# Attention with beacons and a max-out feed-forward on one core: a new order of the opening, behind the first weight's request

## The chip, the cores and the metric

The kernel runs on one core of a Trainium2 chip. The time is the device time of one launch in microseconds; a time for a kernel is the median of several launches. A profile is one more execution of the same program, taken by the hardware profiler; its span is counted from the first to the last recorded instruction and is a little shorter than the time measured around it.

## The reference

```python
B, H, S, Nb, D = 8, 8, 576, 16, 64            # q, k, v, beacon_k, beacon_v: float32
k_all = concat([beacon_k, k], axis=2)          # 16 beacons ahead of the 576 keys
v_all = concat([beacon_v, v], axis=2)
scores = q @ k_all.T / sqrt(D)                 # per batch and head
scores[:, Nb:] is masked causally (the beacons are open to every query)
a = exp(scores - max);  a /= a.sum(-1) + 1e-9
x = (a @ v_all) -> [B * S = 4608 tokens, H * D = 512]
h = max(x @ w1, x @ w2, x @ w3)                # 512 -> 768
out = h @ w_out                                # 768 -> 512, float32
```

The kernel computes with bf16 operands and float32 sums, and takes no maximum ahead of the exponential.

## The kernel before, in words

**Units of work.** A *pair* is two heads of one batch (four pairs a batch, 32 in all; pairs 0 to 3 are batch 0), a *quad* is two pairs. For a pair the q and the k have to stand with the 64 elements of a head along the partitions (tiles `qT` and `kT`, the two heads in the two halves of 64 partitions). For that q and k are loaded, brought to bf16, turned by TensorE transposes into PSUM and copied out. Batch 0 is turned in halves of 288 tokens (step "half": transposes, L435, and copies, L443; its arguments name the engine that copies q, VectorE copies k, and two counts of dummy transposes that `fill` puts ahead, L403). Batch 1 is turned in whole pairs (step "whole": transposes L384, copies of k L459 and of q L448). Each pair's `kT` also gets its 16 beacon columns (steps "keys", L455, from the tile `bT`, which the beacons' transposes in `turn_beacons`, L355, fill).

**Scores, exponential, mask, values.** Step ("scores", p, gi, n) issues n *spare* matmuls that multiply a constant tile by itself (`spare`, L473: they compute nothing that is used), then the six or fewer score matmuls of one of the pair's four groups (L509), then the exponential on ScalarE (L524) into the pair's `at_sb`. Group 0 of a batch 0 pair holds the first 288 queries, groups 1 to 3 the others. Step "mask" zeroes what the causal mask closes in that group: on VectorE by a product with a triangle (L541), on GpSimd by an affine select (L543). Step ("values", quad, half, ...) needs all masks of the quad's two pairs in that half; its matmuls (L584) multiply by a ones tile for the sums and by `v_sb` for the values. ("values", 0, 0) is thus the first half of batch 0's first four heads, ("values", 1, 0) of its other four, ("values", 0, 1) the second half. Then "invert" (logarithm and exponential of the negative on ScalarE, L604 and L606) and "multiply" (VectorE, L616) bring the quotient to `xT`.

**Feed-forward.** A step ("ffn", bank, kind) issues the next unit of a kind: kinds 0 and 1 are the two halves of the first block of 512 tokens times one of the three first weights (`mm1_halves`, L665; VectorE casts the first weight's result and takes the maximum with the second's and third's, L673, L675), kind 2 is the product with w_out. Kind 0 has nine units: three with each weight, w1 first. The later blocks use `mm1_unit` (L646) and `mm2_unit` (L682).

**PSUM.** Scores and turned tiles go through a ring of two tiles `sc`, from the step "widen" on of three; two banks `pv` and, until "widen", two of `fps` ("ffn") carry values, units and turned halves.

**Loads.** SyncE's DMA queue (SP below) is fed in program order with fp32 loads: batch 0's v in five pieces of 128, 128, 128, 128 and 80 rows (`load_v_tile`, beacons L272, v L275), each with its own cast to bf16 (`cast_first_v`, L323), the beacons of batch 1 to 3 (`load_beacons`, L346, cast by "cast keys 1"), batch 1's v in two pieces (three transfers and two, and a transfer of its beacons; cast by "cast v" on GpSimd, L311), and from pair 8 on q and k (`load_pair`, L202 and L207, cast on GpSimd, L255). GpSimd's DMA queue carries what is cast on the way: batch 0's quads by halves (L236), batch 1's quads (L245), each weight in two halves of 384 KB (`load_w`, L333) and w_out (L340). A load with a *gate* ("dve" or "pool") has a tiny memset on that engine ahead of it (L198, L290, L296, L339), which the load waits for: the load can go out only when that engine has come to that place in its own queue.

**What sets the order.** The order is written out by hand: the list `first_steps`, about 170 steps for the opening up to the end of ("whole", 9), then `loop_steps`. The dict `steps` maps each name to a function that issues instructions, under `tc.manual_schedule()`; each engine then executes its own instructions in the order of the list, and waits by semaphores for the others. Two of the functions with what sets a gate and the filler:

```python
def load_first_v(t, gate=None):
    dst = v_stage(0, t)
    if gate:
        idle[gate].memset(dst[32:33, 0, 0:1], 0.0)   # L296: the load waits for this engine's place
    load_v_tile(0, t, dst)

def emit_scores(p, gi, idle=0, now=True):
    ...
    ps = next_tile()
    spare(ps[:, 0], idle)
```

Of the kernel before, what the change touches and what calls it, by code (L numbers as in the profile page):

```python
# [16 lines left out]
def kernel(  # L17
# [141 lines left out]
    ring = [(sc_psum, "sc"), (sc_psum, "sc")]  # L159
# [684 lines left out]
    def start_late():  # L844
# [112 lines left out]
        ("mask", 1, 2, "dve"),  # L957
        ("ffn", "ffn", 0),
        ("mask", 0, 2, "pool"),
        ("scores", 1, 3, 0),  # L960
        ("half", 2, 1, "pv", "act", 0, 0),
        ("scores", 1, 1, 0),
        ("ffn", "ffn", 0),
        ("mask", 1, 3, "pool"),
        ("half", 3, 1, "pv", "dve", 0, 0),
        ("scores", 2, 3, 0),
# [12 lines left out]
        ("ffn", "ffn", 0),  # L979
        ("mask", 3, 3, "pool"),  # L980
        ("load v", 1, 0, "pool"),
        ("mask", 2, 3, "pool"),
        ("invert",),
        ("keys", 5, "act"),
        ("scores", 2, 1, 0),
        ("mask", 2, 2, "pool"),
        ("multiply",),
        ("ffn", "ffn", 0),
        ("mask", 2, 1, "pool"),
        ("mask", 3, 2, "pool"),  # L990
        ("ffn", "ffn", 0),
        ("scores", 3, 1, 1),
# [7 lines left out]
        ("scores", 4, 2, 1),  # L1000
        ("whole", 5, "ring", "act"),
        ("ffn", "ring", 1),
        ("mask", 4, 1, "dve"),
        ("ffn", "ring", 1),
        ("scores", 5, 0, 1),
        ("scores", 4, 0, 0),
        ("load pair", 8, "dve"),
        ("scores", 4, 3, 0),
        ("ffn", "pv", 1),
        ("ffn", "ring", 0),  # L1010
        ("ffn", "pv", 1),
        ("scores", 5, 3, 0),
        ("load pair", 9, "pool"),
        ("mask", 5, 0, "dve"),
        ("mask", 4, 2, "dve"),
        ("mask", 5, 3, "dve"),
        ("scores", 5, 2, 0),
        ("load quad", 1, 1),
        ("mask", 4, 3, "dve"),
        ("keys", 7, "act"),  # L1020
        ("scores", 5, 1, 0),
        ("mask", 4, 0, "pool"),
        ("ffn", "pv", 0),
        ("ffn", "ring", 0),
# [5 lines left out]
        ("mask", 5, 2, "pool"),  # L1030
        ("cast v", 1, 0),
        ("scores", 6, 2, 0),
        ("scores", 6, 1, 0),
        ("mask", 5, 1, "pool"),
        ("scores", 6, 0, 0),
        ("load w_out", "dve"),
        ("ffn", "pv", 1),
        ("load", 1),
        ("values", 2, 0, "ring", 0, 4, 0),
        ("invert",),  # L1040
        ("keys", 9, "act"),
        ("cast pair", 8),
        ("whole", 7, "ring"),
        ("mask", 6, 0, "pool"),
        ("ffn", "pv", 1),
        ("multiply",),
        ("cast pair", 9),
        ("load", 2, "dve"),
        ("scores", 6, 3, 0),
        ("scores", 7, 2, 0),  # L1050
        ("cast v", 1, 1),
        ("whole", 8, "pv", "dve"),
        ("load", 1, "pool"),
        ("scores", 7, 0, 0),
        ("mask", 6, 1, "dve"),
        ("mask", 7, 0, "dve"),
        ("mask", 6, 3, "dve"),
        ("scores", 7, 1, 0),
        ("mask", 7, 1, "pool"),
        ("mask", 7, 2, "pool"),  # L1060
        ("values", 2, 1, "ring", 0, 4, 0),
        ("keys", 8, "pool"),
        ("invert",),
        ("mask", 6, 2, "dve"),
        ("scores", 7, 3, 0),
        ("load", 1, "dve"),
        ("whole", 9, "ring", "act"),
        ("multiply",),
        ("mask", 7, 3),
        ("load", 1),  # L1070
        ("ffn", "pv", 1),
    ]
    loop_steps = [
        ("late",),
# [586 lines left out]
```

## Time and profile before

| | |
|---|---|
| median of 3 launches | 291.97 us (291.77 to 292.08) |
| profiled execution, measured around it | 292.01 us |
| its span | 289.6 us |
| granted clock of TensorE, mean | 0.999 |
| HBM read and written | 35.13 MB and 9.44 MB |
| transfers by SP's queue (q1) | 39.20 MB |
| transfers by GpSimd's queue (q0) | 5.21 MB |

All times in what follows are microseconds from the start of the span. In the lists of stretches each line gives the stretch, its length, and then for TensorE's matmuls, its weight loads, VectorE, ScalarE and GpSimd the busy time with the number of instructions in brackets, then the granted clock, and the transfers' rate at the end. In a timeline each line gives the start, the length, the engine, the line of the kernel, the operation with output and inputs, the shapes and the count of like instructions, and in square brackets the wait ahead of it with what ended it. Of several releasers the list names the one that came last. In the list of transfers, the number behind the KB is the time from request to landing.

The opening touched by the change lies between 10.3 us (the requests of w1, which go out at 10.74 and 11.29) and about 57.6 us (the end of ("whole", 9) and the unit behind it). These are the transfers of that stretch, by the trace's records of request and of last landing:

| transfer | queue | requested | landed |
|---|---|---|---|
| batch 0, v pieces 0, 1, 2 | SP | 6.25, 6.61, 7.21 | 9.66, 10.62, 11.59 |
| w1, two halves | GpSimd | 10.74, 11.29 | 17.69, 19.61 |
| batch 0, second quad, second half | GpSimd | 13.64, 14.34 | 20.45, 21.32 |
| v piece 3 | SP | 16.80 | 22.28 |
| beacons of batches 1 to 3 | SP | 17.2 to 18.3 | 22.45 to 22.84 |
| v piece 4 | SP | 21.07 | 23.96 |
| w2, two halves | GpSimd | 21.45, 21.99 | 27.19, 29.12 |
| batch 1, first quad, q and k | GpSimd | 24.49, 25.19 | 30.49, 31.99 |
| w3, two halves | GpSimd | 27.07, 27.62 | 33.85, 36.01 |
| batch 1, v pieces 0 to 2 | SP | 29.77, 30.13, 30.73 | 37.14, 40.44, 42.33 |
| batch 1, second quad, q and k | GpSimd | 32.15, 32.85 | 39.48, 42.09 |
| w_out | GpSimd | 48.04 | 59.90 |

### The profile page before, as it was taken

How to read it: one execution, taken by the hardware profiler on the slowest of the kernel's cores; microseconds unless marked ns; L12 is line 12 of the kernel's file. 1: busy time of each engine (PE TensorE's matmuls, PEld its weight loads, DVE VectorE, ACT ScalarE, POOL GpSimd, SP SyncE). 2: the span in 40 equal slices, each digit the busy share in tenths (PEclk: the TensorE clock that was granted, in tenths of full speed). 3: DMA queues.
4: the chain of work that ended last, by engine and by line, in shares of the span. 5: the costliest groups of instructions: out<-in, count | busy, mean ns of one | idle time of the engine just before them, and what ended most of it. 6: DMA issues, size and time to landing. Idle time of an engine off the chain costs nothing.

```text
span 289.6 us, 8831 instructions
## 1 busy us (share of the span) xinstructions
PE 279.8 (97%) x3704; PEld 160.6 (55%) x3729; DVE 168.2 (58%) x317; ACT 145.2 (50%) x248; POOL 121.9 (42%) x246
## 2 busy tenths in 40 slices
PE   8889999999999999999999999999999999999995
PEld 7656677754555554544555887445554545444442
DVE  1555677856675557565746655665556565373273
ACT  2886576854566564835484258525862552200300
POOL 3717416644476483638365546464523320000000
PEclk9999999999999999999999999999999999999999
DMA  8999999999999999999999999999991003002103
GB/s 131 168 179 183 219 198 234 221 205 219 235 204 187 148 197 164 199 170 219 201 181 157 223 192 194 139 167 187 253 163 75 2 2 144 3 0 82 65 0 146
DMA packets 118231, 45.30 MB, mean 156 GB/s; under 512 B 107312, under 2 KB 112944, under 8 KB 118192
## 3 DMA queue, kind: packets, MB, share of 16 engines
q1 hardware_dynamic: 111984, 39.20, 76.1%
q0 software_dynamic: 5648, 5.21, 11.9%
q8 instruction: 29, 0.48, 0.7%
q10 hardware_dynamic: 560, 0.33, 0.4%
q14 instruction: 10, 0.08, 0.1%
HBM read 35.13 MB, written 9.44 MB: 154 GB/s over the span
## 4 chain that ended last, share of the span: by engine, by line
PE 86%; DMA 4%; ACT 3%; DVE 2%; POOL 2%; issue 1%; ACTq 0%; POOLq 0%
PE pv L646 21%; PE sc L646 14%; PE wide L646 8%; PE sc L682 8%; PE sc L584 7%; PE pv L682 6%; PE sc L509 6%; PE pv L584 5%; PE wide L509 3%; DMA w_sb<-in_moe_w_dram 2%; DMA bk<-in_beacon_k_dram 2%; PE wide L682 1%; PE pv L665 1%; PE wide L584 1%; PE sc L665 1%
## 5 line engine op out<-in xcount | busy, mean ns | idle before, releaser
L524 ACT ACTIVATE at_sb<-sc 128x736 bf16<-128x736 f32 (+5 forms) x87 | 72.9, 863 | 62.9 <-PE sc L509 62.3
L543 POOL TENSOR_SCALAR_AFFINE_SELECT at_sb<-at_sb 128x256 bf16<-128x256 bf16 (+3 forms) x140 | 51.7, 387 | 105.7 <-ACT at_sb L524 104.7
L646 PEld LDWEIGHTS <-w_sb 128*128 128x128 bf16 x648 | 61.1, 98 | 60.7 <-issue 4.9
L646 PE MATMUL pv<-xT,w_sb 128*128 128x512 bf16 (+1 forms) x315 | 65.2, 347 | 0.3
L524 ACT ACTIVATE at_sb<-wide 128x672 bf16<-128x672 f32 (+3 forms) x41 | 35.1, 856 | 23.3 <-PE wide L509 23.1
L646 PE MATMUL sc<-xT,w_sb 128*128 128x512 bf16 (+1 forms) x202 | 44.1, 362 | 0.3
L656 DVE TENSOR_TENSOR hT<-hT,pv 128x512 bf16<-128x512 bf16 x48 | 32.4, 686 | 13.2 <-PE pv L646 13.2
L255 POOL CAST p<-st 96x768 bf16<-96x768 f32 x48 | 38.3, 824 | 3.4 <-DMA st<-in_k_dram 3.4
L682 PEld LDWEIGHTS <-hT 128*128 128x128 bf16 x210 | 19.6, 98 | 23.5 <-issue 1.1
L616 DVE TENSOR_TENSOR xT<-pv,recip 128x288 bf16<-128x288 f32 (+2 forms) x48 | 14.2, 350 | 26.5 <-ACT recip L606 26.5
L509 PE MATMUL sc<-qT,kT 64*128 64x288 bf16 (+6 forms) x286 | 26.8, 271 | 2.0 <-POOL at_sb L543 0.6
L509 PEld LDWEIGHTS <-kT 64*128 64x128 bf16 x400 | 14.8, 94 | 22.2 <-issue 12.8
L646 PE MATMUL wide<-xT,w_sb 128*128 128x512 bf16 (+1 forms) x113 | 26.1, 364 | 0.5 <-issue 0.2
L584 PEld LDWEIGHTS <-v_sb 128*32 128x32 bf16 (+1 forms) x1408 | 24.7, 96 | 2.3 <-issue 1.0
L682 PE MATMUL sc<-w_out_sb,hT 128*128 128x512 bf16 x103 | 24.4, 379 | 0.3
L656 DVE TENSOR_TENSOR hT<-hT,sc 128x1024 bf16<-128x1024 bf16 (+1 forms) x15 | 17.0, 1147 | 5.2 <-PE sc L646 5.0
L682 PE MATMUL pv<-w_out_sb,hT 128*128 128x512 bf16 x83 | 19.9, 380 | 0.1
L656 DVE TENSOR_TENSOR hT<-hT,wide 128x1024 bf16<-128x1024 bf16 (+1 forms) x11 | 12.3, 1120 | 10.8 <-PE wide L646 10.6
L311 POOL CAST v_sb<-st 128x1536 bf16<-128x1536 f32 (+2 forms) x21 | 18.4, 896 | 0.0
L654 DVE CAST hT<-pv 128x512 bf16<-128x512 f32 x20 | 13.7, 688 | 5.0 <-PE pv L646 5.0
L694 DVE COPY y<-sc 128x1024 f32<-128x1024 f32 (+1 forms) x10 | 11.2, 1118 | 8.7 <-PE sc L682 8.7
L616 DVE TENSOR_TENSOR xT<-sc,recip 128x288 bf16<-128x288 f32 (+2 forms) x39 | 11.5, 351 | 7.9 <-ACT recip L606 7.9
(115 smaller groups left out, 280.7 us busy)
## 6 DMA issues: line engine op xcount, KB each, us to landing
st<-in_q_dram SPq DMA_DIRECT2D x24, 288.0 KB, 5.6
st<-in_k_dram SPq DMA_DIRECT2D x24, 288.0 KB, 6.2
st<-in_v_dram SPq DMA_DIRECT2D x24, 256.0 KB, 5.8
out_dram<-y SPq DMA_DIRECT2D x9, 512.0 KB, 4.6
out_dram<-y SPq DMA_DIRECT2D x17, 256.0 KB, 3.0
w_sb<-in_moe_w_dram POOLq DMA_DIRECT2D x6, 384.0 KB, 7.0
st<-in_v_dram SPq DMA_DIRECT2D x8, 224.0 KB, 5.4
st<-in_v_dram SPq DMA_DIRECT2D x8, 160.0 KB, 4.3
```

The source lines that it names most:

```text
L255: cast(t16.rearrange("p r h d -> p h r d"), st[0:QP, i * NQ2 : (i + 1) * NQ2].rearrange("p (h r d) -> p h r d", h=2, r=QR),)
L311: cast(v_sb[0:n, t:t1].rearrange("p t h d -> p (t h d)"), st[0:n, (t - t_lo) * H * D : (t1 - t_lo) * H * D],)
L509: nc.tensor.matmul(ps[:, e, off : off + q1 - q0], kT[hs, 128 * t : 128 * t + 128], qT[hs, q0:q1], start=True, stop=True, tile_position=(64 ...
L524: nc.scalar.activation(out=both_heads(p, gi), in_=ps[:, :, 0 : g_width(p, gi)], func=AF.Exp, scale=scale)
L543: nc.gpsimd.affine_select(out=view, in_=view, compare_op=ALU.is_ge, fill=0.0, base=x0, pattern=[[0, 2], [1, hi - lo]], channel_multiplier=-1,)
L584: nc.tensor.matmul(ps[bank][32 * j : 32 * j + 32, lo + q0 - qa : lo + qb - qa], lhsT, at_view(PPQ * quad + j // 2, t, j % 2, q0, qb), star ...
L616: nc.vector.tensor_mul(xT[:, 2 * g + part - 1, c0 + ca : c0 + cb], ps[bank][:, lo : lo + cb - ca], recip[:, ca:cb],)
L646: nc.tensor.matmul(dst[:, o0 : o0 + n], w_in[i][:, ct, 128 * (ft + f) : 128 * (ft + f + 1)], xT[:, ct, x0 : x0 + n], start=(ct == 0), stop ...
L654: (by_act if alone[0] else by_dve)(h, ps)
L656: nc.vector.tensor_max(h, h, ps)
L682: nc.tensor.matmul(ps[:, t - tt] if two else ps, hT[:, ft, 128 * t : 128 * (t + 1)], w_out_sb[:, ft, :], start=(ft == 0), stop=(ft == n_ft ...
L694: nc.vector.tensor_copy(y[:, 0:n], ps if two else ps[:, None])
```

## The change

Only the list `first_steps` is touched, and of it only what stands behind ("load w", 0); the steps ahead of it, the loop and all functions are the same. No arithmetic of the result is added or left out. In words:

- *Batch 0's v.* Pieces 0 and 1 are cast on ScalarE (GpSimd and VectorE before), piece 2 on VectorE (ScalarE before), piece 3 on ScalarE and piece 4 on VectorE (both GpSimd before). Piece 3 is requested earlier, gated by VectorE ahead of piece 2's cast; piece 4 is gated by VectorE behind the second "multiply", and now stands ahead of the beacons of batches 1 to 3 on SP's queue.
- *Masks.* Many change between VectorE and GpSimd; pair 2's first mask goes from VectorE to GpSimd.
- *Weights on GpSimd's queue.* w2 ("load w", 1) is requested behind w1's first unit and ahead of a mask of pair 0's group 3; before, it was behind a mask of pair 0's group 1 on GpSimd. w3 stands behind batch 1's first quad as before.
- *Batch 1.* Its first quad and, without a gate, its first v piece are requested together behind ("values", 0, 1); before, the quad stood further ahead and the v had a gate on GpSimd further behind. The beacons of batches 1 to 3 are cast by VectorE (GpSimd before) and turned behind the "invert" of these values. Beacon columns of pairs 4, 7 and 8 are copied by GpSimd, of 6 by VectorE. Pair 6 is turned two feed-forward units earlier in TensorE's order, with ScalarE in place of VectorE for the copy of q.
- *Loads of pairs 8 and 9* are gated by GpSimd (VectorE and GpSimd before) and stand earlier. w_out loses its gate.
- *Filler.* 23 spare matmuls become 19, in other places, and six dummy transposes are added ahead of pair 2's first half.

The diff's core (three dots on a line mark what is left out, which is the rest of the opening from pair 5's masks on, where only masks, "load" and "keys" change places):

```diff
         ("load w", 0),
-        ("cast v0", 0, "pool"),
+        ("mask", 0, 0, "dve"),
+        ("cast v0", 0, "act"),
         ("half", 3, 0, "ffn", "act", 0, 0),
-        ("mask", 0, 0, "dve"),
-        ("cast v0", 1, "dve"),
-        ("half", 2, 0, "pv", "dve", 4, 0),
-        ("cast v0", 2, "act"),
-        ("scores", 3, 0, 3),
+        ("cast v0", 1, "act"),
         ("mask", 1, 0, "pool"),
-        ("scores", 2, 0, 6),
+        ("half", 2, 0, "pv", "act", 4, 3),
+        ("scores", 3, 0, 4),
+        ("load v0", 3, "dve"),
+        ("cast v0", 2, "dve"),
+        ("scores", 2, 0, 4),
+        ("mask", 3, 0, "dve"),
         ("values", 0, 0, "pv", 0, 4, 0),
+        ("invert",),
+        ("load quad half", 1, 1),
         ("half", 0, 1, "ffn", "act", 0, 7),
-        ("invert",),
-        ("load v0", 3, "dve"),
-        ("scores", 0, 2, 4),
-        ("mask", 3, 0, "dve"),
-        ("mask", 2, 0, "dve"),
+        ("scores", 0, 2, 2),
         ("scores", 0, 3, 0),
+        ("mask", 2, 0, "pool"),
         ("multiply",),
         ("values", 1, 0, "ffn", 0, 4, 0),
         ("invert",),
         ("half", 1, 1, "pv", "act", 0, 0),
         ("multiply",),
-        ("scores", 0, 1, 0),
-        ("mask", 0, 3, "dve"),
-        ("load quad half", 1, 1),
+        ("load v0", 4, "dve"),
+        ("scores", 0, 1, 1),
         ("scores", 1, 2, 0),
+        ("mask", 0, 2, "dve"),
+        ("ffn", "ffn", 0),
+        ("mask", 0, 1, "dve"),
+        ("load w", 1),
+        ("mask", 0, 3, "pool"),
+        ("scores", 1, 3, 0),
+        ("ffn", "ffn", 0),
         ("load keys 1",),
-        ("load v0", 4, "dve"),
-        ("mask", 0, 1, "pool"),
+        ("mask", 1, 2, "pool"),
+        ("scores", 1, 1, 0),
+        ("half", 2, 1, "pv", "dve", 0, 0),
         ("ffn", "ffn", 0),
-        ("load w", 1),
...
+        ("scores", 2, 3, 0),
+        ("scores", 2, 2, 7),
+        ("scores", 3, 2, 0),
+        ("cast v0", 3, "act"),
+        ("cast v0", 4, "dve"),
+        ("mask", 3, 2, "dve"),
+        ("mask", 1, 1, "pool"),
+        ("scores", 3, 3, 0),
+        ("values", 0, 1, "pv", 0, 4, 0),
+        ("load quad", 1, 0),
+        ("load v", 1, 0),
+        ("load w", 2),
+        ("invert",),
+        ("cast keys 1", "dve"),
+        ("turn keys 1",),
         ("ffn", "ffn", 0),
...
-        ("cast v0", 3),
-        ("load quad", 1, 0),
-        ("scores", 2, 2, 7),
-        ("cast v0", 4),
-        ("scores", 3, 2, 0),
-        ("mask", 1, 1, "dve"),
-        ("cast keys 1", "pool"),
-        ("values", 0, 1, "pv", 0, 4, 0),
-        ("scores", 3, 3, 0),
-        ("load w", 2),
-        ("turn keys 1",),
-        ("keys", 4, "act"),
         ("ffn", "ffn", 0),
...
         ("whole", 4, "ffn", "dve"),
+        ("keys", 4, "pool"),
         ("widen",),
+        ("load pair", 8, "pool"),
+        ("keys", 5, "act"),
         ("values", 1, 1, "pv", 0, 4, 0),
...
-        ("load v", 1, 1),
-        ("load", 2, "dve"),
-        ("whole", 6, "ring", "dve"),
-        ("keys", 6, "pool"),
+        ("whole", 6, "ring", "act"),
+        ("ffn", "ring", 0),
+        ("ffn", "ring", 0),
+        ("load", 1, "dve"),
         ("ffn", "pv", 1),
...
```

More of the change, by code (lines that the diff above doesn't have):

```diff
@@ L1002 @@
         ("ffn", "ring", 1),
-        ("mask", 4, 1, "dve"),
         ("ffn", "ring", 1),
-        ("scores", 5, 0, 1),
+        ("mask", 4, 2, "dve"),
+        ("load pair", 9, "pool"),
+        ("scores", 5, 0, 0),
         ("scores", 4, 0, 0),
-        ("load pair", 8, "dve"),
-        ("scores", 4, 3, 0),
-        ("ffn", "pv", 1),
+        ("ffn", "pv", 1),
+        ("load quad", 1, 1),
+        ("mask", 5, 0, "dve"),
+        ("keys", 7, "pool"),
+        ("keys", 6, "dve"),
+        ("scores", 4, 3, 0),
@@ L1030 @@
[L1030 to L1038, printed above, removed]
+        ("mask", 5, 3, "pool"),
+        ("mask", 5, 2, "pool"),
+        ("scores", 6, 2, 0),
+        ("scores", 6, 0, 0),
+        ("load w_out",),
+        ("scores", 6, 1, 0),
+        ("mask", 4, 0, "dve"),
+        ("mask", 6, 2, "dve"),
@@ L1039 @@
+        ("ffn", "pv", 1),
         ("values", 2, 0, "ring", 0, 4, 0),
+        ("cast pair", 8),
+        ("keys", 9, "act"),
+        ("mask", 6, 0, "pool"),
         ("invert",),
[L1041 to L1044, printed above, removed]
+        ("whole", 7, "ring", "act"),
+        ("load", 2, "pool"),
+        ("cast v", 1, 1),
         ("ffn", "pv", 1),
         ("multiply",),
-        ("cast pair", 9),
-        ("load", 2, "dve"),
+        ("load", 1, "dve"),
@@ L1061 @@
[L1061 to L1069, printed above, removed]
+        ("values", 2, 1, "ring", 0, 4, 0),
+        ("cast pair", 9),
+        ("invert",),
+        ("whole", 9, "ring", "act"),
+        ("mask", 7, 0, "pool"),
+        ("multiply",),
+        ("scores", 7, 3, 0),
+        ("mask", 6, 3, "pool"),
@@ L1070 @@
+        ("ffn", "pv", 1),
+        ("mask", 7, 1, "pool"),
+        ("mask", 7, 3, "pool"),
         ("load", 1),
-        ("ffn", "pv", 1),
     ]
```

61 lines of the change are left out of this document (22 added, 39 removed).

## The prediction

> **What bounds the kernel now.** I read the page first, then the stretches of 10 us, then the timeline of TensorE, of the other engines, and last the transfers. The page and two stretches:
>
> ```profile
> span 289.6 us, 8831 instructions
> ...
> PE 279.8 (97%) x3704; PEld 160.6 (55%) x3729; DVE 168.2 (58%) x317; ACT 145.2 (50%) x248; POOL 121.9 (42%) x246
> ```
>
> ```profile
> 10.00:20.00 10.00, 8.60 (x200) 5.46 (x200) 5.72 (x20) 7.68 (x14) 5.02 (x10) 1.00 1.18 165
> ...
> 40.00:50.00 10.00, 9.44 (x160) 7.23 (x159) 7.01 (x17) 6.49 (x10) 4.95 (x9) 1.00 1.04 220
> 50.00:60.00 10.00, 9.42 (x225) 7.04 (x223) 7.41 (x21) 8.86 (x16) 5.83 (x14) 1.00 1.16 223
> ```
>
> TensorE (first pair of numbers after the length) is the bound. From 10 to 60 us, all that the new order touches, it is busy 46.58 of 50 us: 3.4 us of open waits, and some filler matmuls that compute nothing. From 60 us on the waits view names no wait of TensorE above 0.2 us, so an opening that is shorter by x ends the kernel x earlier, and the order cannot win more than those 3.4 us and its filler. Here are the waits, in TensorE's timeline (start, length, line, tiles, count, in brackets the wait and what ended it):
>
> ```profile
> 11.82 0.40 PE L509 MATMUL sc<-qT,kT 64*128 64x288 bf16 x6 [0.17 <-ACT qT L443]
> ...
> 13.74 0.40 PE L509 MATMUL sc<-qT,kT 64*128 64x288 bf16 x6 [0.61 <-POOL at_sb L543]
> ...
> 17.63 0.59 PE L584 MATMUL fps<-at_sb,ones 128*32 128x288 bf16 x12 [0.43 <-DVE at_sb L541]
> ...
> 20.77 1.91 PE L665 MATMUL fps<-xT,w_sb 128*128 128x256 bf16 x16 [0.26 <-DVE xT L616]
> ...
> 29.17 0.83 PE L665 MATMUL fps<-xT,w_sb 128*128 128x256 bf16 x6 [0.24 <-DMA w_sb<-in_moe_w_dram]
> ...
> 47.18 0.53 PE L509 MATMUL sc<-qT,kT 64*128 64x464 bf16 x6 [0.56 <-DVE qT L448]
> ```
>
> **The change, stage by stage.** Times are the profiled execution's, 292.01 us outside for a span of 289.6, and 0.04 above the median 291.97; I subtract from the median.
>
> *10.3 to 15.4 us, the first values.* ScalarE now casts two v pieces (0.64 each, from its cast at 11.64) between the second exponential (ends 11.47) and the copies of qT for pairs 3 and 2. Pair 3's scores slip from 11.82 to 12.4. GpSimd loses its v cast (0.63 at 11.83), so pair 1's mask ends at 13.1, not 13.68; pair 2's scores come at 13.35 and values (0,0) at 13.65 instead of 14.07. The filler goes from 23 matmuls of 0.14 to 19, with six transposes of 0.02 more; most lies inside waits. **-0.4.**
>
> *To the first feed-forward unit (20.77).* Pair 2's mask moves from VectorE, where it ended with pair 3's at 17.89, to GpSimd: pair 2's exponential ends near 15.1, the three selects take 1.29 (row at 12.40), done at 16.4. Values (1,0) follow the scores at 16.6, not 17.63. The chain from there (values, logarithm, reciprocal, product) leads to 19.55; the first weight's second half, requested at 11.29, lands 8.3 later, at 19.6. So this unit starts at 19.6: **-0.75 more, -1.15 in all.**
>
> *To values (0,1) and the beacons (28.5).* From the first unit to values (0,1) TensorE needed 5.82. In the new order pair 3's last scores (0.13) stand ahead of these values and wait for the exponential of (2,2), about 0.5; and v piece 3 is cast on ScalarE behind the exponential of (3,2), done near 27.2, where the values need it at 26.9: 0.25. Values end near 28.0 against 28.34 with the same work: **+0.8, -0.35 in all.** The second weight is requested not at 21.45, behind a mask that waited 6.07 for ScalarE, but at 16.5, behind pair 2's mask. Unit 4, which took 1.40 with its wait (28.53 to 29.93), then takes 0.92: **-0.48, -0.83 in all.**
>
> *What the earlier weight costs.* The piece that I cannot see in the old trace: v piece 4 (requested at 20.0, gated by a VectorE write after the product) and the beacons of batches 1 to 3, now behind it on SP's queue (20.3 to 21.8 instead of 17.2), meet a busy transfer path. Before, GpSimd's queue was empty when they came. From the transfers view, each line of a window of its own (KB, us from request to landing):
>
> ```profile
> st<-in_v_dram SPq DMA_DIRECT2D x1, 160.0 KB, 2.9
> ...
> w_sb<-in_moe_w_dram POOLq DMA_DIRECT2D x2, 384.0 KB, 7.6
> ...
> st<-in_v_dram SPq DMA_DIRECT2D x1, 224.0 KB, 7.4
> ```
>
> The first is v piece 4 at 21.07. The second is the third weight at 27.07 and 27.62 (6.8 and 8.4, landing at 33.9 and 36.0). The third is batch 1's v, requested at 29.77: it lands at 37.1, after that weight, though such a piece took 3.4 when asked for near 6.5. That is the order of request, across queues. Taken so: batch 0's last quad half landed at 21.3 (14.34 + 7.0); v piece 3, now requested near 12.3 ahead of it, pushes it by 1.0 (it landed at 22.3, 1.0 after the quad). The weight then takes 4.0 (the third one, 32.0 to 36.0) to 4.8 (the second, 24.3 to 29.1), so it is in at 26.3 to 27.1. Piece 4 adds 0.6 (160 KB at piece 3's rate), the beacons (96 KB in three) 0.5: 26.9 to 27.7, and 27.4 to 28.2. VectorE's cast (0.41) ends at 27.3 to 28.1; the values want it at 27.2. Bounds of the stall: 0 if piece 4 lands by 26.8, 0.9 at the late end; I take 0.5, the middle. Behind the waiting cast on VectorE stand a mask of pair 3, wanted only by values (1,1), and the beacons' cast (0.4), for which TensorE's beacon transposes wait after the values: hidden while these run on for 0.8. **+0.5, -0.33 in all.**
>
> [...]
>
> *To the end of values (1,1) (35.37).* One filler (0.23, 32.01 to 32.24) goes; exponential, mask and the two copies of pair 4 that TensorE waits for follow in the same lengths. Batch 1's first quad is requested at 23.5 and 24.2 (24.49 and 25.19 before), with the first piece of batch 1's v ahead of it: by the order above its keys land near 32, wanted at 32.3. Hidden. **-0.25, -0.6 in all.**
>
> *To 57.57, the end of the new order.* Pair 6 is turned two units earlier, ScalarE instead of VectorE copies its q, and three units stand between turn and scores: the gap before 47.18 (unit at 45.58 of 0.88, so 0.7 lost) goes, as does the filler at 38.57 (0.14). What is late next: pair 7's scores wait for ScalarE's copy as before (0.30 at 51.84). Beacon copies of 0.2 change engines, off the path; pairs 8 and 9 and the rest of v are requested 4 to 7 us earlier on SP. GpSimd's cast of batch 1's v (1.47) holds the masks of pair 5 behind it while it waits for its transfers; both are wanted only by values (2,0), some 8 us after the cast can start. **-0.8, -1.4 in all.**
>
> Sum: 291.97 - 1.4 = **290.6 us**.
>
> **Rivals.**
>
> (A) *Small pieces are passed over, slower.* If GpSimd's queue goes on with batch 1's first quad (in reach of the engines at about 25, before the weight is done) ahead of v piece 4, two transfers of 1.4 and 1.5 (30.5 to 32.0) stand before it: it lands near 30.2, VectorE stands still in its cast and TensorE in values (0,1), 2.9 longer than taken: -1.4 + 2.9 = +1.5, 293.5 us. It decides from a landing at 28.7 on (27.3 taken, plus 1.4), and is beyond 0.2% at 29.3. For it: from 24 to 33 us nearly all packets are GpSimd's. Against: nothing of SP was asked for in most of that time, and 29.77 landed right after what was asked before it. Chance 0.24.
>
> (B) *The small pieces get turns between the weight's rows.* Piece 4 then takes 2.9 (its own row) to 5.5 (piece 3, asked for at 16.80 with GpSimd's transfers in flight): 22.9 to 25.5, before 26.8. No stall: -1.9, 290.1 us. Against: 29.77's piece. Chance 0.14. [...]
>
> (C) *Batch 1's v beside its quad eats the rest.* Its two other pieces (about 1.0 each; 10.3 and 11.6 us from request to landing before) get in front of the quad's keys or of the second quad, which pair 6 wants two units earlier: up to 1.2 of stall, -0.2, within 0.2%: 291.8. For it: SP asks for them from 22.4 on. Against: when two were pending, SP's third request took 2.49 to go out (30.73), so they would come behind the quad. Chance 0.20.
>
> **How the numbers follow.** Likeliest, 0.42: 290.6, own range 290.0 to 291.3. With B on the same side, faster is 0.56; C is same, 0.20; A slower, 0.24. The bound of 0.2% is 0.58 us, against 0.31 between the lowest and highest run (291.77, 292.08). Low end 289.8: B, and the 0.30 at 51.84 gone too. High end 292.9: C and the nearer half of A, where piece 4 lands between 28.7 and 29.6.
>
> **What would show it.** In the changed profile: values (0,0) near 13.65, the first unit near 19.6, GpSimd's second weight request near 16.5; VectorE's 80-row v cast with a wait for its transfer that ends near 27.4; the third stage right if the values on tile pv run 26.1 to 28.5; no wait for VectorE's qT near 46. The forecast is wrong if that cast begins after 28.7, if the beacons' transposes wait, or if the turning of pairs 4 or 6 waits for a transfer.

## The result: slower, 294.22 against 291.92 us

The changed kernel takes 294.22 us (median of 10 runs, 292.18 to 295.27), the kernel before 291.92 (291.38 to 292.97): a ratio of 1.0058, 95% interval 1.0040 to 1.0077. (The ratio and its interval, here and below, are taken over all runs of both kernels; the quotient of the two medians alone would be 1.0079 here.) The forecast was 290.6, faster by 1.4. The times also spread over 3.1 us where those before spread over 1.6. The profiled execution was one of the shorter ones, 292.51 us with a span of 290.5; a second profile of the same kernel, taken in the first series below, has 293.53 and 291.5, nearer to the usual run.

The page of the changed kernel, and the stretches of 10 us:

```profile
span 290.5 us, 8835 instructions
...
PE 280.3 (96%) x3706; PEld 160.4 (55%) x3731; DVE 167.2 (58%) x311; ACT 146.5 (50%) x249; POOL 120.5 (41%) x251
```

```profile
10.00:20.00 10.00, 9.20 (x210) 5.64 (x209) 5.08 (x20) 9.46 (x18) 6.82 (x15) 1.00 1.15 164
20.00:30.00 10.00, 8.39 (x155) 5.65 (x155) 5.06 (x13) 6.56 (x12) 4.08 (x9) 1.00 1.26 202
...
40.00:50.00 10.00, 9.53 (x144) 6.98 (x142) 7.20 (x18) 6.96 (x10) 4.95 (x9) 1.00 1.05 191
50.00:60.00 10.00, 9.09 (x208) 6.68 (x198) 6.89 (x18) 8.78 (x15) 5.82 (x15) 1.00 1.17 228
```

The second stretch in the kernel before:

```profile
20.00:30.00 10.00, 9.32 (x167) 6.47 (x168) 4.93 (x13) 7.04 (x14) 6.92 (x15) 1.00 1.05 180
```

TensorE gains 0.6 of busy time in the stretch from 10 us (8.60 before) and loses 0.9 in the next (9.32 before) and 0.3 in the last (9.42). Its timeline names the waits:

```profile
12.45 0.40 PE L509 MATMUL sc<-qT,kT 64*128 64x288 bf16 x6 [0.42 <-ACT qT L443]
...
19.73 0.38 PE L665 MATMUL fps<-xT,w_sb 128*128 128x256 bf16 x2 [0.26 <-DVE xT L616]
20.59 0.83 PE L665 MATMUL fps<-xT,w_sb 128*128 128x256 bf16 x6 [0.48 <-DMA w_sb<-in_moe_w_dram]
...
27.11 0.30 PE L509 MATMUL sc<-qT,kT 64*128 64x288 bf16 x2 [0.72 <-ACT at_sb L524]
...
29.51 0.27 PE L355 MATMUL sc<-ident,bk 48*128 48x48 bf16 x4 [0.41 <-DVE bk L876]
...
44.52 0.45 PE L384 MATMUL sc<-ident,whole 96*64 96x96 bf16 x12 [0.47 <-DMA whole<-in_k_dram]
...
52.29 0.37 PE L509 MATMUL sc<-qT,kT 64*128 64x464 bf16 x2 [0.30 <-ACT qT L448]
...
59.89 0.55 PE L584 MATMUL pv<-at_sb,v_sb 128*32 128x288 bf16 x25 [0.57 <-issue]
```

The waits that the order was said to remove are gone: 0.61 ahead of pair 2's scores, 0.43 ahead of values (1,0), 0.24 at unit 4, 0.56 ahead of pair 6's scores. Six others have come or grown: for ScalarE's copy at pair 3's first scores (0.17 before), for the first weight, for a ring tile at pair 3's last scores, for the beacons' cast, for batch 1's second quad, and near 60 us a wait that the profile puts down to no other engine ("issue", 0.17 before). In the second profile (TensorE's timeline again) the wait for issue is larger, that for the beacons is about the same, those for the first weight and the second quad are not there, and one for the cast of v piece 4 is added:

```profile
29.40 0.73 PE L584 MATMUL pv<-at_sb,v_sb 80*32 80x80 bf16 x40 [1.23 <-DVE v_sb L323]
30.50 0.27 PE L355 MATMUL sc<-ident,bk 48*128 48x48 bf16 x4 [0.37 <-DVE bk L876]
...
60.93 0.55 PE L584 MATMUL pv<-at_sb,v_sb 128*32 128x288 bf16 x25 [1.28 <-issue]
```

The waits account for most of the time. Summed from 9.8 to 100 us as the timelines list them, against the 3.10 of the kernel before: 3.63 in the first profile (+0.53, span +0.95) and 4.79 in the second (+1.69, span +1.99). The remaining 0.4 and 0.3 are in no listed wait.

Why do loads come late? The transfers views of the stretch from 20 to 24 us, first of the kernel before, then of the changed one (packets, MB, share of 16 engines; q1 is SP's queue, q0 GpSimd's):

```profile
q1 hardware_dynamic: 1801, 0.44, 55.8%
q0 software_dynamic: 152, 0.19, 33.2%
```

```profile
q0 software_dynamic: 468, 0.74, 100.5%
q1 hardware_dynamic: 390, 0.10, 16.6%
```

Before, GpSimd's queue ran nearly empty there (4 packets from 21 to 23 us): the last quad half had landed at 21.32, and the second weight was asked for only at 21.45. In that gap SP's pieces of v and the beacons went through, 1801 small packets. In the changed kernel the second weight (requested at 16.03; 16.5 forecast) fills the gap, SP moves 390 packets, and v piece 3 lands at 24.89 though it was asked for 4.5 us sooner (22.28 before), piece 4 at 27.60 (28.83 in the second profile), and the beacons at 28.85. Most of the 390 (267) went out in the first microsecond, when GpSimd's queue still had the last quad's packets of 384 bytes; from 22 to 24 us, beside the weight's rows of 3072 bytes, SP moved 66 of its 256-byte packets, and a v piece of 128 rows has 1024 of them:

```profile
q0 software_dynamic: 155, 0.40, 102.4%
q1 hardware_dynamic: 66, 0.02, 6.1%
```

### The profile page after: what moved, and what is told of

Read it like the earlier page. It is cut to its first block, busy times and chain, and to the rows that moved or that the text cites. A ratio compares the mean times of both kernels' runs of the same rounds, so it can differ in the third digit from the quotient of the medians.

```text
span 290.5 us, 8835 instructions
## 1 busy us (share of the span) xinstructions
PE 280.3 (96%) x3706; PEld 160.4 (55%) x3731; DVE 167.2 (58%) x311; ACT 146.5 (50%) x249; POOL 120.5 (41%) x251
## 4 chain that ended last, share of the span: by engine, by line
PE 85%; DMA 8%; ACT 2%; issue 1%; DVE 1%; POOL 0%; SPq 0%; ACTq 0%; DVEq 0%
PE pv L646 21%; PE sc L646 14%; PE wide L646 8%; PE sc L682 8%; PE sc L584 7%; PE pv L682 6%; PE sc L509 6%; DMA bk<-in_beacon_k_dram 4%; PE pv L584 4%; DMA whole<-in_k_dram 4%; PE wide L509 3%; PE pv L665 2%; PE wide L682 1%; PE wide L584 1%; PE sc L393 1%
## 5 line engine op out<-in xcount | busy, mean ns | idle before, releaser
L524 ACT ACTIVATE at_sb<-sc 128x736 bf16<-128x736 f32 (+5 forms) x86 | 72.1, 868 | 61.7 <-PE sc L509 60.2
L543 POOL TENSOR_SCALAR_AFFINE_SELECT at_sb<-at_sb 128x256 bf16<-128x256 bf16 (+3 forms) x144 | 52.5, 382 | 107.6 <-ACT at_sb L524 105.7
L524 ACT ACTIVATE at_sb<-wide 128x672 bf16<-128x672 f32 (+3 forms) x42 | 35.8, 851 | 23.2 <-PE wide L509 23.0
L682 PEld LDWEIGHTS <-hT 128*128 128x128 bf16 x210 | 19.6, 98 | 23.5 <-issue 1.1
L616 DVE TENSOR_TENSOR xT<-pv,recip 128x288 bf16<-128x288 f32 (+2 forms) x48 | 14.2, 351 | 27.3 <-ACT recip L606 27.3
```

Of the source, the lines that this page charges most:

```text
L524: nc.scalar.activation(out=both_heads(p, gi), in_=ps[:, :, 0 : g_width(p, gi)], func=AF.Exp, scale=scale)
L543: nc.gpsimd.affine_select(out=view, in_=view, compare_op=ALU.is_ge, fill=0.0, base=x0, pattern=[[0, 2], [1, hi - lo]], channel_multiplier=-1,)
L616: nc.vector.tensor_mul(xT[:, 2 * g + part - 1, c0 + ca : c0 + cb], ps[bank][:, lo : lo + cb - ca], recip[:, ca:cb],)
L682: nc.tensor.matmul(ps[:, t - tt] if two else ps, hT[:, ft, 128 * t : 128 * (t + 1)], w_out_sb[:, ft, :], start=(ft == 0), stop=(ft == n_ft ...
```

## The experiments

Each ratio is to runs of the kernel before on the same chip in the same series, since its own median moved between 291.9 and 292.6 from series to series.

### One request back at a time

The changed kernel once more:

> The changed kernel once more, for a second profile, since its ten times lie between 292.18 and 295.27 (before: 291.38 to 292.97) and the profile at hand shows a run of 292.51, near the lower end. Three theories on what is late. P (pairs 8 and 9): their q and k are requested at 32.8 to 36.7 in place of 39.5 to 41.8 and share the transfer path with batch 1's second quad, whose k landed at 44.48 (42.09 before) where pair 6's transposes wait for it, 0.47. V (batch 0's v, rival A of the prediction): v piece 4 (27.60) and the beacons of batches 1 to 3 (28.85) land behind the earlier second weight; values (0,1) and the beacons' turning wait. Q (rival C): batch 1's v beside its first quad delays that quad and itself. All three expect a median of 293.5 to 294.5. In a profile of 293.5 or more, P expects the quad's k at 45.5 or later and the wait grown to 1.5 or more, V the beacons' turning at 30.5 or later, Q the first quad's k behind 33.2.

Measured: 293.32, ratio 1.0043 (1.0019 to 1.0068). The profile is the one shown above: v piece 4 and the beacons are late (V), the first quad's k lands at 33.78 (Q), the second quad's at 44.34 without a wait. P's mark, 45.5 or later, is not met. The median is a little below the 293.5 that all three expected at least.

Pair 8's load back:

```diff
-        ("load pair", 8, "pool"),
...
         ("scores", 4, 0, 0),
+        ("load pair", 8, "dve"),
```

> The changed kernel with the load of pair 8 back behind the scores of pair 4's group 0 and gated by VectorE, as before; pair 9 and the rest of batch 1's v follow it on SP's queue, so all are requested from about 40 on. P: the second quad's k lands near 42, pair 6's transposes do not wait, 1.0 to 2.0 us faster than the changed kernel (292.2 to 293.2). V and Q: no difference, 294.0 within 0.4.

Measured: 293.53, ratio 1.0043 (1.0023 to 1.0063). No wait at pair 6 (the k lands at 43.88), and no gain in time. But the edit moved less than was expected of it. Pair 9's load, gated by GpSimd, stands ahead of pair 8's new place in the list, so that pair 9 now goes out first and early, and only pair 8 and the rest of v go out late. SP's timeline has pair 9 and then pair 8:

```profile
34.05 0.33 SPq L202 DMA_DIRECT2D st<-in_q_dram  x1
34.43 1.21 SPq L202 DMA_DIRECT2D st<-in_k_dram  x1
41.59 0.31 SPq L202 DMA_DIRECT2D st<-in_q_dram  x1
```

In the kernel before, the two went out at 39.51 and 41.31, in the changed one at 32.79 and 35.16. So P is tested for one pair of the two only, here and in the runs below that use this edit. The profile also has a stretch at half clock (last section).

The second weight one step later:

```diff
-        ("load w", 1),
         ("mask", 0, 3, "pool"),
+        ("load w", 1),
```

> The changed kernel with the second weight's request one step later, behind pair 0's mask of group 3 on GpSimd: near 21 instead of 16.0. V: v piece 4 and the beacons land 2 us earlier or more (25.5 and 26.5), values (0,1) and the beacons' turning do not wait, 1.0 to 2.0 us faster (292.2 to 293.2), less up to 0.5 if unit 4 then waits for the weight. P and Q: not faster, 294.0 to 294.7.

Measured: 293.60, ratio 1.0062 (1.0038 to 1.0086). The edit was too small to test anything: GpSimd reached that place at 18.13, not 21, and v piece 4 still landed at 27.96.

Batch 1's first v piece back:

```diff
-        ("load v", 1, 0),
...
         ("mask", 3, 3, "pool"),
+        ("load v", 1, 0, "pool"),
```

> The changed kernel with the first piece of batch 1's v taken from beside its quad: behind pair 3's mask of group 3, gated by GpSimd, as before (near 29 instead of 21.8 to 26.7). Q: the first quad and the third weight land about 1 us earlier and the second quad up to 1 us, 0.7 to 1.5 us faster (292.7 to 293.5). P and V: within 0.4 of the changed kernel.

Measured: 293.00, ratio 1.0033 (1.0009 to 1.0057). The first quad's k lands at 31.78, 0.9 earlier, and the third weight at 35.79, 1.6 earlier, as Q has it; the time lies in Q's interval, but most of the loss stays. None of these edits alone gains more than 0.1%, less than the intervals, so none of the three theories is shown to carry the loss by itself.

### Several requests back, and single ones in the kernel before

Two requests back, then all five:

```diff
-        ("load v0", 3, "dve"),       
...
         ("mask", 2, 0, "pool"),
         ("multiply",),
+        ("load v0", 3, "dve"),
...
-        ("load w", 1),
         ("mask", 0, 3, "pool"),
...
         ("mask", 1, 2, "pool"),
+        ("load w", 1),
```

> The changed kernel with two requests of the opening back near their old times: v piece 3 gated behind the first product (near 17 instead of 12.2), the second weight behind pair 1's mask of group 2 (near 21.2 instead of 16.0; 18.1 was too little, with v piece 4 still at 27.96). Theory R (requests moved forward push what is wanted sooner): the first weight's second half lands at 19.6 (20.3 to 20.8 in four of the five profiles) and unit 1 does not wait (0.46 to 1.05); v piece 4 lands before 26, the beacons before 27, and neither values (0,1) (0 to 1.23) nor the beacons' turning (0.37 to 0.41) wait; in all 1.0 to 1.8 faster than the changed kernel: 291.8 to 292.8. Theory O (the order of work is at fault: the 0.72 ahead of pair 3's last scores in all profiles, and the wait for issue near 60, 0.57 to 1.28): within 0.4 of the changed kernel, 293.2 to 294.2.

Measured: 293.37, ratio 1.0032 (1.0009 to 1.0055). v piece 4 now lands at 24.35 and the last of the beacons at 27.77 (28.85 in the changed kernel), and neither the values nor the beacons' turning wait: R's mechanism is there. Its amount is not: the time lies in O's interval, above R's. In the profiled execution (294.65, the longest of the twelve) other waits are long: 1.28 for the first weight, 0.51 for the first quad and 1.72 for the second, here in TensorE's timeline:

```profile
46.10 0.45 PE L384 MATMUL sc<-ident,whole 96*64 96x96 bf16 x12 [1.72 <-DMA whole<-in_k_dram]
```

R's mark for the first weight, 19.6, was not met either: its second half landed at 21.16, with v piece 3 asked for at its old time.

> The changed kernel with all five moved requests near their old times: v piece 3 and the second weight as in the run above, batch 1's v behind pair 3's mask gated by GpSimd, pair 8 gated by VectorE, w_out gated by VectorE. R: as the run above, and another 0.3 to 0.8 from the second quad (0.47 in one profile) and from a shorter wait near 60: 291.0 to 292.2, at the kernel before or below it. O: 0.72 and the wait near 60 stay, 293.0 to 294.0.

```diff
-        ("load w_out",),
+        ("load w_out", "dve"),
```

With this, the two edits above, and batch 1's v and pair 8 as in the first series, all five requests are back near their old times; everything else of the new order stays, and with it pair 9's early load (34.44, 41.31 before). Measured: 291.09, ratio 0.9968 (0.9948 to 0.9989): faster than the kernel before, inside R's interval and far from O's. This settles the direction: the new order of the engines' work is a gain (0.9 us by this ratio, 0.3 to 1.5 by its interval), and the requests moved forward, taken together, turn it into a loss. SP's queue moves 1496 packets from 20 to 24 us again. The 0.72 ahead of pair 3's scores and a wait for issue (1.09) stay, so O was right about two terms, but they are not what decides.

The reverse, one request moved forward in the kernel before:

```diff
         ("load quad half", 1, 1),
+        ("load w", 1),
...
         ("ffn", "ffn", 0),
-        ("load w", 1),
```

> The kernel before with the second weight's request alone moved forward, behind batch 0's last quad half on GpSimd (near 15 instead of 21.45). R: v piece 4, requested at 21, lands near 27 instead of 23.96; its cast on GpSimd then ends near 28, where values (0,1) want it at 27.3: 0.3 to 1.0 of wait, less the 0.48 of unit 4's wait for that weight: 292.0 to 292.8 (before: 292.0). The prediction's likeliest case, with the wait at 0.5, expects 292.0; its case B (small pieces slip in, v piece 4 at 25.5 or sooner) 291.5.

Measured: 293.61, ratio 1.0060 (1.0032 to 1.0088): this one line costs as much as the whole change. TensorE's timeline and GpSimd's:

```profile
29.37 0.73 PE L584 MATMUL pv<-at_sb,v_sb 80*32 80x80 bf16 x40 [1.48 <-POOL v_sb L323]
```

```profile
26.77 0.61 POOL L323 CAST v_sb<-st 128x512 bf16<-128x512 f32 x1 [2.62 <-DMA st<-in_v_dram]
27.32 0.70 POOL L245 DMA_DIRECT2D whole<-in_q_dram  x1
28.01 0.69 POOL L245 DMA_DIRECT2D whole<-in_k_dram  x1
28.68 0.63 POOL L323 CAST v_sb<-st 80x512 bf16<-80x512 f32 x1
29.24 0.63 POOL L876 CAST bk<-bk 48x512 bf16<-48x512 f32 x1
29.79 1.10 POOL L333 DMA_DIRECT2D w_sb<-in_moe_w_dram  x2
```

v piece 3, requested at 16.95, lands at 26.64 (22.28 before), just behind the weight's 25.99; GpSimd stands 2.62 in its cast, the quad's requests and piece 4's cast are queued behind it, and TensorE waits 1.48. SP moves 578 packets from 20 to 24 us. The wait of 0.24 for the weight is gone as promised. The time is above R's range, and the late piece is piece 3, where R had piece 4. Part of the way to the wait is this kernel's own: here GpSimd casts the pieces, and its waiting in that cast delays the first quad's requests to 27.32 (24.49 before), while in the changed kernel ScalarE and VectorE cast them. So the run shows what this request can cost alone, not what share it has in the changed kernel's loss.

```diff
         ("cast v0", 1, "dve"),
+        ("load v0", 3, "dve"),
...
         ("invert",),
-        ("load v0", 3, "dve"),
```

> The kernel before with the request of v piece 3 alone moved forward, gated by VectorE behind its cast of piece 1 (near 12.3 instead of 16.80). R: the first weight's second half lands 0.7 to 1.2 later than 19.61, and the first unit (20.77) waits up to 0.3 for it: 292.0 to 292.4; the piece itself lands no sooner than 22. The prediction (requests served in their order, piece 3 pushes the quad, not the weight) expects the weight at 19.6 and no difference, 292.0 within 0.2.

Measured: 292.44, ratio 1.0008 (0.9994 to 1.0022): no difference that this can tell. In the profiled execution the piece, requested at 12.83, landed at 24.42, 2.1 later than when asked for at 16.80; the first weight's second half at 21.14 and the quad's k at 24.15 made TensorE wait 0.22 and 0.83. So R's direction shows in the landings, and its price in the time is small.

### Which of the later requests

> The changed kernel with v piece 3, the second weight and the first piece of batch 1's v at their old requests; pair 8, pair 9 and w_out stay early. It stands between the run with two requests back (293.4, with 0.51 for the first quad and 1.72 for the second in its profile) and that with all five back (291.1). Theory Q (batch 1's v beside its quad is what was left): near 291.1 to 291.8, no wait at the turning of pair 4, and the second quad's k before 43.5. Theory P (pairs 8 and 9 are): 292.5 to 293.4, the second quad's k at 44.5 or later and its wait still there.

The edits are those of the run with two requests back and of the one with batch 1's v back. Measured: 291.86, ratio 0.9990 (0.9968 to 1.0011). No wait at pair 4, and the second quad's k at 43.06 without a wait: Q's marks, with a time 0.06 above its range.

> The same, with pair 8 gated by VectorE as before, and batch 1's v left beside its quad. P: 291.1 to 291.8, the second quad's k before 43.5. Q: 292.5 to 293.4, with the wait at the turning of pair 4 (0.5) and some at that of pair 6. If the two prices add up, both runs stand near 292.2.

Here batch 1's v stays early and pair 8's edit takes its place. Measured: 292.16, ratio 1.0013 (0.9992 to 1.0035). The wait at the turning of pair 4 is there (0.43), the second quad's k lands at 42.73 without a wait. From the run with two requests back (1.0032), batch 1's v is worth 0.0042, pair 8 0.0019, and with w_out all of it 0.0064: the prices add up, though the intervals are about as wide as the prices, and pair 9 stays early in all these runs.

> The kernel before with batch 1's first v piece alone moved forward, behind its first quad in the order and without a gate (SP asks near 22 to 25 instead of 29.77). The prediction's case C: the quad's keys (31.99) or the second quad land later and cost up to 1.2: 292.2 to 293.2. The prediction's likeliest case: hidden, 292.0 within 0.2.

```diff
         ("load quad", 1, 0),
+        ("load v", 1, 0),
...
-        ("load v", 1, 0, "pool"),
```

Measured: 292.70, ratio 1.0022 (1.0000 to 1.0044). The quad's k lands at 34.21 (31.99 before) and pair 4's turning waits 0.49; the second weight's wait grows from 0.24 to 0.41. Case C has its mechanism, at some 0.6 us by the ratio, with an interval from 0 to 1.3.

### The waits that stayed

```diff
-        ("scores", 3, 3, 0),
         ("values", 0, 1, "pv", 0, 4, 0),
+        ("scores", 3, 3, 0),
```

> The changed kernel with all five requests back, and pair 3's last scores behind values (0,1) again. The 0.72 ahead of these scores (a tile of the ring that the exponential still reads, in all profiles) should go: 0.4 to 0.7 faster than the run with five requests back (291.1), 290.4 to 290.7. If the values then wait for a mask, a cast or v piece 4 in its place, no gain: 291.1 within 0.3.

On top of the five requests. Measured: 291.28, ratio 0.9962 (0.9938 to 0.9986): no gain over 0.9968. The 0.72 is gone, and in the values stands 0.92 for ScalarE's cast of v piece 3, which is queued behind the exponential of pair 3's group 2 although the piece had landed at 23.22. That is the second outcome written down. TensorE's row and ScalarE's:

```profile
28.00 0.82 PE L584 MATMUL pv<-at_sb,v_sb 128*32 128x208 bf16 x44 [0.92 <-ACT v_sb L323]
```

```profile
27.33 0.62 ACT L323 CAST v_sb<-st 128x512 bf16<-128x512 f32 x1
```

```diff
+        ("cast v0", 3, "act"),
         ("scores", 2, 3, 0),
         ("scores", 2, 2, 7),
         ("scores", 3, 2, 0),
-        ("cast v0", 3, "act"),
```

> The changed kernel with all five requests back, pair 3's last scores behind values (0,1), and v piece 3 cast by ScalarE ahead of the exponential of pair 2's group 3 (it landed at 23.2, and ScalarE stands idle at 24). If the 0.72 ahead of the scores and the 0.92 in the values that took its place are both ScalarE's order, values (0,1) run from 26.0 without a wait: 0.5 to 0.9 faster than the two runs before it (291.1 and 291.3), 290.3 to 290.7. If another wait follows (v piece 4's cast on VectorE, the beacons), 291.0 to 291.4.

Measured: 290.48 (median of 8), ratio 0.9927 (0.9903 to 0.9951); both kernels are beaten. Its page and its TensorE's timeline:

```profile
span 288.4 us, 8863 instructions
```

```profile
25.80 0.68 PE L584 MATMUL pv<-at_sb,ones 128*32 128x288 bf16 x20
26.30 1.18 PE L584 MATMUL pv<-at_sb,v_sb 128*32 128x288 bf16 x56
27.41 0.30 PE L509 MATMUL sc<-qT,kT 64*128 64x288 bf16 x2
27.87 0.27 PE L355 MATMUL sc<-ident,bk 48*128 48x48 bf16 x4 [0.16 <-DVE bk L876]
...
28.99 0.83 PE L665 MATMUL fps<-xT,w_sb 128*128 128x256 bf16 x6 [0.52 <-DMA w_sb<-in_moe_w_dram]
...
57.97 0.55 PE L584 MATMUL pv<-at_sb,v_sb 128*32 128x288 bf16 x25 [0.25 <-issue]
```

Values (0,1) run from 25.80 without a wait. The listed waits sum to 1.91, 1.19 less than in the kernel before, and the span is 1.2 shorter. Against the 3.18 of the run before this one, the 0.92 is what the cast's new place took away; 0.74 for the second quad's k and 0.20 for the first weight stood in that profile and not in this one, and 0.16 for the beacons and 0.52 for the second weight came in.

### By what rule the two queues share the path

```diff
+        n = 2 if i == 1 else 1
         for g in range(n_quad):
-            nc.gpsimd.dma_start(
-                out=w_in[i][:, 2 * g : 2 * g + 2, f0:f1], in_=wv[g, :, :, f0:f1]
-            )
+            for x in range(n):
+                a, b = f0 + (f1 - f0) * x // n, f0 + (f1 - f0) * (x + 1) // n
+                nc.gpsimd.dma_start(
+                    out=w_in[i][:, 2 * g : 2 * g + 2, a:b], in_=wv[g, :, :, a:b]
+                )
```

> The changed kernel, with the second weight's two transfers cut into four by columns, so that its packets are 1536 bytes, not 3072; nothing else. Theory T (the engines take turns between the two queues, a packet each: in the profile of the changed kernel SP's 256-byte packets go one for one beside GpSimd's, 254 with 268 packets in the microsecond from 19, 50 to 65 a microsecond beside the weight, and 552 once that queue runs dry): twice as many turns while the weight passes, so v piece 3 (24.89) lands 1.5 to 3 us sooner, the weight (26.94) 0.5 to 1.5 later, and v piece 4 (27.60), which comes last either way, within 0.8 of its old place; time within 0.6 of the changed kernel (293.0 to 294.0). Theory F (transfers are served in the order of request, as the prediction had it): piece 3 and piece 4 within 0.5 of their old landings.

Measured: 293.74, ratio 1.0046 (1.0018 to 1.0074), as the changed kernel. (The turns that the expectation reads from the changed kernel, 254 with 268, were beside the last quad's 384-byte packets. In the microseconds from 21, 22 and 23 us, as the weight's 3072-byte rows take over, SP had 57, 26 and 40 packets, GpSimd 111, 89 and 66.) The weight's packets came out at 768 bytes, not 1536, four times as many as before the cut. It landed at 29.06 (2.1 later), piece 3 at 24.07 (0.8 sooner), piece 4 at 28.12. (Its profiled execution, 297.21, has two stretches at half clock; its length is not compared.) That meets neither theory: T wanted piece 3 1.5 us sooner at least, F wanted it unmoved. SP's queue of this run, from 22 to 24 us, did not get a packet for each of GpSimd's (123 beside 524), while in the changed kernel from 19 to 20 us, beside the quad's packets, it did:

```profile
q0 software_dynamic: 524, 0.36, 119.5%
q1 hardware_dynamic: 123, 0.03, 11.5%
```

```profile
q0 software_dynamic: 267, 0.10, 81.9%
q1 hardware_dynamic: 268, 0.07, 52.1%
```

What stays open is why SP gets a packet for each of GpSimd's in one place and far fewer in another. That its small packets get through when GpSimd's queue is nearly empty (1125 beside 4 from 21 to 23 us in the kernel before), and slowly beside its weights (66 beside 155 from 22 to 24 us in the changed one), is shown.

## Why the prediction was wrong, point by point

- *TensorE is the bound; waits from 10 to 60 us are what can be won.* Right. The sums of listed waits follow the spans from profile to profile within 0.4 us, wherever the clock stayed up. The signs of being wrong that the prediction named came too: the beacons' transposes waited in both profiles of the changed kernel, pair 6's turning in the first, and v piece 4's cast began at 28.92 in the second.
- *First values at 13.65, values (1,0) at 16.6, first unit at 19.6.* The order's part was right: 13.76, 16.66, 19.73. The unit then waited 0.48 for the weight's second half, which landed at 20.55, not 19.6. The step took its old flight of 8.3 us although two quad transfers and v piece 3 were asked for sooner; in the profiles of the changed kernel and of the first series it took 8.6 to 9.7. Piece 3 is not the whole reason: with it back at its old time the half took 8.5 to 9.9.
- *Pair 3's last scores wait about 0.5; v piece 3's cast is done near 27.2.* Right in kind: 0.72, and a cast from 27.61 to 28.23. The two are one thing, ScalarE's queue, as the last runs showed.
- *What the earlier weight costs: +0.5, against -0.48 at unit 4.* This is the step that failed: the price of asking for the loads sooner. The sum takes +0.5 for the weight, which its -0.48 cancels, and nothing for v piece 3, batch 1's v, pairs 8 and 9 and w_out. The runs showed about +0.0075 to +0.0090 of the time, 2.2 to 2.6 us, for the five together (1.0043 and 1.0058 against 0.9968 with them back). For v piece 4 the landing was nearly as worked out in the first profile (27.60; 27.3 forecast), and the values did not wait for it; it was 28.83 in the second, where the wait was 1.23, above the bound of 0.9. In the kernel before, the weight's request alone cost 0.6% (some 1.6 to 1.8 us) where the step's two terms cancel. The price was taken as a queue of transfers served in the order of request. The runs showed that SP's 256-byte packets went through in the gap on GpSimd's queue (1801 packets of SP from 20 to 24 us before, 390 in the changed kernel), and that v piece 3, asked for 4.5 us sooner but beside a weight, landed later (24.89; 22.28 before). How much of the changed kernel's loss is the weight's and how much that of the later requests stays open: with the weight and v piece 3 back the ratio fell only from 1.0043 to 1.0032, within the intervals.
- *The beacons' turning is hidden.* Wrong, 0.41 and 0.37: they land at 28.85 and 29.91, behind v piece 4, and VectorE's cast of them (28.97 to 29.45, 30.03 to 30.45) ends some 0.3 behind the values.
- *Rival B, turns between the weight's rows and no stall.* The runs bear even turns out in part: from 19 to 20 us, beside the quad's 384-byte packets, SP had 268 packets beside GpSimd's 267. The estimate of no stall was wrong: v piece 4 landed at 27.60 and 28.83, not at 22.9 to 25.5, and the values waited 1.23 for its cast in the second profile. A turn of 256 bytes against one of 3072 is a small share of the bytes, so that turns by packet would make the small pieces late, not early. Where SP got 66 packets beside 155, or 123 beside 524, the trace does not agree with even turns.
- *Pair 6's gap goes, 0.8 gained.* The 0.56 did go. In its place came 0.47 for the second quad's k (44.48 against 42.09). Pairs 8 and 9 requested 4 to 7 us earlier were listed and costed at nothing, with no cover named; together with batch 1's v they push that quad, by 1.72 of wait in one profile (with either pair 8 or batch 1's v back, its k landed at 42.73 and 43.06).
- *Rival A, slower by passing over the small pieces.* Its sign came true and nearly its time (293.5 forecast for it), and a landing beyond 28.7 was seen. Its agent was wrong: not batch 1's quad, which landed at 32.2 and 33.8 in that profile, but the weight itself; and the 2.9 of stall at v piece 4 that it priced was 0 and 1.23. That its time came close is luck.
- *Rival C.* Its mechanism is there, alone worth 1.0022 (1.0000 to 1.0044), where the prediction gave it as an alternative to the others; these costs came on top of each other. The order alone was sized within the interval: 1.4 us of gain would be a ratio of 0.9952, and 0.9968 (0.9948 to 0.9989) was measured.

## What to carry to other kernels

A request moved forward isn't free because its own wait goes: ask which gap on the transfer path it fills and what used that gap, and look at the packets of both queues there, not at the landing of the moved transfer alone. Where a change moves both the engines' order and several requests, price them apart: here the order alone was worth -0.3%, the requests +0.75 to +0.9%. A cast queued on an engine behind a wait of another kind can be late even though its data are there (v piece 3 had landed at 23.22 and was cast from 27.33); moving it into the idle time ahead took away a wait of 0.92, and the ratio went from 0.9962 to 0.9927 (two series, with intervals that overlap a little). And read in the new profile what an edit really moved: a load put back behind another in a hand-written list can send the other one out first.

## What the runs showed of the hardware

**The clock fell to half after four of the waits.** In three of the profiles TensorE's granted clock fell to half in the midst of the kernel, four times in all, each time for 3.41 us, after waits of 1.05, 1.72, 1.22 and 2.15. The stretches of 2 us of the run with pair 8's load back, whose wait of 1.05 ended at 20.87 (third column from the right is the clock):

```profile
20.00:22.00 2.00, 1.13 (x9) 0.62 (x10) 0.26 (x1) 0.44 (x1) 0.32 (x1) 0.91 1.25 205
22.00:24.00 2.00, 2.00 (x12) 1.16 (x12) 0.71 (x3) 0.65 (x1) 0.00 (x0) 0.50 1.11 211
24.00:26.00 2.00, 2.00 (x26) 1.25 (x22) 1.43 (x3) 1.00 (x1) 0.49 (x2) 0.73 1.16 219
```

Eight matmuls of a unit took 1.89 there instead of 1.05. That run's waits sum to 0.64 more than before and its span is 2.0 longer, so the drop cost about 1.4, an estimate. Waits of 1.23, 1.28, 1.48 and 1.53 in other profiles were followed by none. In the 3.41 us just ahead of the four drops TensorE's matmuls were busy 1.98, 1.70, 1.81 and 1.53 us, 45 to 58%. The length of the wait does not tell the drops from the rest (one followed 1.05 and 1.22, none 1.53); what does was not shown, and no run moves a wait to test it. The stretch ahead of the drop shown (the drop begins at 21.66), with TensorE's matmuls alone:

```profile
18.25:21.66 3.41, 1.98 (x19) 1.00 1.31 194
```

Such drops may be part of the wider spread, but not all of it: of the ten timed runs of the changed kernel three had a mean clock of 0.994 or less, and the longest (295.27) had 0.999.

**A wait of TensorE goes with a packet of instructions.** The wait "for issue" near 60 us stands at the same matmul in every profile of this order that has it, the one with 25 left of its pass; it measured 0.25 to 1.53, and 0.16 to 0.45 in the kernel before and its variants. By the trace's packet records one 16 KB packet of the instruction queue (the page's q8) starts 2.4 to 3.0 us ahead of the end of that wait, wherever that falls (56.92 and 59.89 in the first profile, 58.15 and 60.93 in the second, 56.37 and 58.91 with all five requests back). That the wait is for this packet, and that the packet is late because of the loads in flight, is the author's guess; no run moved it by itself.
